# Vertical output matmuls as pairs of 128 rows by 64 columns

## The chip, the core and the metric

The kernel runs on one core of a Trainium2 chip. The metric is the device time of one execution in microseconds (us); lower is better. The core has five engines with queues of their own: TensorE (PE, matmuls, with its weight loads shown as PEld), VectorE (DVE), ScalarE (ACT), GpSimd (POOL) and SyncE (SP, which issues most of the DMAs). They run in parallel and wait for one another by semaphores.

## The reference: attention in horizontal and vertical stripes

An image of 224 x 224 tokens with 96 channels goes through one projection to q, k and v. The first 48 channels attend within horizontal stripes of 8 rows, the last 48 within vertical stripes of 8 columns; each kind has 28 stripes of 1,792 tokens. Both results are joined and multiplied by the output matrix `wo`.

```python
qkv = einsum('bhwc,cd->bhwd', x, wqkv)          # x 1x224x224x96, wqkv 96x288
# per horizontal stripe, channels 0..47; nh = 28 stripes of 8*224 tokens
ah = softmax(einsum('bqc,bkc->bqk', qh, kh) * 48**-0.5)
oh = einsum('bqk,bkc->bqc', ah, vh)
# per vertical stripe, channels 48..95; the same with qv, kv, vv -> ov
o  = concat(oh, ov)                              # written as two pads and a sum
return einsum('bhwc,cd->bhwd', o, wo)            # wo 96x96
```

Because `wo` acts on the 48 + 48 channels separately, the output is `oh @ wo[:48] + ov @ wo[48:]`. The kernel uses this: it finishes the horizontal part first, keeps it in SBUF, and adds it to the vertical part.

## The kernel before

**Tiling.** Two stripes are worked on together as a pair; there are 28 pairs, P = 0 to 13 horizontal and P = 14 to 27 vertical. Stripe w = 0 of a pair lives in partitions 0 to 63 and stripe w = 1 in partitions 64 to 127 of the tiles `QT_sb`, `KT_sb` and `OT_sb`. A pair's queries are cut into four chunks, of 512, 512, 512 and 256.

**Scores.** A unit is 128 keys by 512 queries (or twice 128 keys by 256) for both stripes of the pair. `qk_op` (L1015) computes a unit's scores with matmuls of 48 rows by 128 columns. In this text "rows" of a matmul are the partitions over which it sums, and "columns" the partitions of PSUM that it writes; the profile prints them as `48*128`. The two stripes' matmuls sit in different halves of the array's rows and are issued as a pair.

**Exponentials.** ACT takes 1,071 units with one activation each (L1037, PSUM to `PT`). DVE takes the other 301 (L1075 to L1094), with a part of the products on POOL.

**Values.** `pv_op` (L968) multiplies the probabilities by `V_sb`, with matmuls of 128 rows by 64 columns (`128*64` in the profile): stripe 0 writes PSUM partitions 0 to 63, stripe 1 partitions 64 to 127, and the two are again issued as a pair. `V_sb` has a column of ones behind the 48 channels, so row 48 of each result is the sum of the exponentials. DVE copies a finished chunk to `OT_sb` (L931).

**Output.** `fin` multiplies `OT_sb` by `wo`. For horizontal pairs (L809) a slot is a block of 64 tokens times one of the two stripes: the matmul has 128 rows by 64 columns and uses `wo_sb[0][w]`, a tile of 128 partitions that holds `wo` in the partitions of stripe w alone and zeros in the others. Two such matmuls, one for each stripe, fill the 128 partitions of a slot, and a group has 4 or 5 slots, so 8 or 10 matmuls of 97 moving columns. For vertical pairs a slot is 128 tokens of one stripe. With `rowed` set (L836, from the constant `VQ`, L372) the slot is a single matmul (L843) that sums over the 49 partitions of its stripe and writes all 128 partitions: `49*128`. A group again has 4 or 5 slots. Then DVE takes the reciprocal of the sums (L796), multiplies (L853), and POOL adds the horizontal part `Ph_sb` (L859); SP writes the output by DMA. One group, the last of all, is not `rowed` and runs as pairs at L847 in the kernel before too.

**Order.** The order of the work is written out as strings in `PLAN`, one for each engine: the string `"pe"` names by a digit the stream from which PE takes its next operation. Digits 1 and 2 are score units for ACT and for DVE, 3 and 4 are value products, 5 is an output group, 6 a projection for the next pair. `PLAN["bank"]` gives the PSUM banks in the same way. A planner (L167 to L343) walks through these strings, keeps an estimated clock, and so finds the waits and the buffers; ACT and SP have no string, and SP takes what the estimated clock has ready first. `mode` is a mark of each PE operation, "q" for the row form (L1018, and L913 for `rowed` groups) and "v" for the others; the planner's clock adds `SWITCH`, 0.099 or 0.117 us, where the mark changes. With the order given, it enters only this estimated clock.

In the string `"pe"`, the digits before and after each of the 84 `rowed` groups read as follows: 65 stand between a score unit and a value product or projection, 17 between two score units, and 2 between a value product and a score unit. None stands between two of the "v" kind.

Of the kernel before, what the change touches and what calls it, by code (L numbers as in the profile page):

```python
# [368 lines left out]
PRIO = (1, 0, 3, 5, 4, 2)  # L369
DPRIO = (0, 1, 2, 3)  # L370
HALVES = False
VQ = True  # L372
HB = [0, 5, 10, 15, 20, 24, 28]
VB = [0, 5, 10, 14]
LEAD, SPACE, PACE, FIRST = 8, 3, 0.9, 0
# [2 lines left out]
def bass_standalone__window_attn_cswin__vision_kernel(  # L378
# [30 lines left out]
    with es:  # L409
# [380 lines left out]
        def fin(P, c):  # L790
# [35 lines left out]
            else:  # L826
# [5 lines left out]
                for (k0, k1), ws in todo:  # L832
                    nk = k1 - k0
                    n = nk * len(ws)
                    last = P == NP - 1 and c == NCH - 1
                    rowed = VQ and len(ws) == 1  # L836

# [386 lines left out]
```

## Time and profile before

| | us |
|---|---|
| median of 3 runs | 1007.16 |
| lowest and highest | 1005.09, 1011.97 |
| the profiled execution | 1004.3 |
| its span, first to last instruction | 1002.5 |
| PE busy | 988.0 (99%) |
| ACT busy | 987.6 (99%) |
| DVE busy | 938.5 (94%) |
| POOL busy | 684.2 (68%) |
| granted TensorE clock | 0.999 of full |

The time of an execution is the span and 1.8 us around it. "Busy" is the union of the times in which an engine has an instruction in flight. Matmuls overlap: one with 512 moving columns is shown as some 380 ns, while the next pair starts some 215 ns after it. So a share of 99% doesn't mean that PE could do no more, and the pace is read from starts in the timeline and not from durations. In a row of the timeline, the first number is the start in us from the beginning of the span, the second how long the row's instructions are in flight together, and xN their count.

### The profile page before, as it was taken

The page shows a single profiled execution, that of the slowest core. Times are in us where ns is not written, and L with a number is a line of the kernel's source. Part 1 is how long each engine was busy: PE and PEld are TensorE (multiplying, and loading weights), DVE is VectorE, ACT ScalarE, POOL GpSimd, SP SyncE. Part 2 cuts the span into 40 slices and gives each one's busy share as a digit, 9 for nine tenths or more (in the row PEclk, how much of TensorE's full clock was granted, in tenths as well). Part 3 has the DMA queues.
Part 4 walks back from the last instruction along what each step waited for, and adds up shares of the span by engine and source line. Part 5 has one row for each costly group of instructions (what it writes and reads, how often), then busy time and mean ns, then how long its engine had stood idle before and what let it go on. Part 6 is the DMA issues. An engine that isn't in the chain of part 4 may idle for free.

```text
span 1002.5 us, 24560 instructions
## 1 busy us (share of the span) xinstructions
PE 988.0 (99%) x10211; PEld 385.9 (38%) x10211; DVE 938.5 (94%) x1573; ACT 987.6 (99%) x1080; POOL 684.2 (68%) x660
## 2 busy tenths in 40 slices
PE   8999999999999999999999999999999999999997
PEld 3433433343343334334334333433433443343342
DVE  8999999999999999999899999999999999999997
ACT  7999999999999999999999999999999999999997
POOL 3676766667677676777776776776676777677652
PEclk9999999999999999999999999999999999999999
DMA  5102120220112023011111122222122221222012
GB/s 110 39 2 38 38 32 8 38 38 1 39 39 32 8 38 38 2 36 25 27 29 32 25 46 50 54 52 44 34 41 52 53 54 39 52 52 40 13 36 50
DMA packets 164712, 36.92 MB, mean 37 GB/s; under 512 B 164488, under 2 KB 164488, under 8 KB 164600
## 3 DMA queue, kind: packets, MB, share of 16 engines
q1 hardware_dynamic: 163016, 34.80, 18.5%
q8 instruction: 80, 1.31, 0.5%
q10 hardware_dynamic: 1584, 0.55, 0.2%
q14 instruction: 32, 0.26, 0.1%
HBM read 0.44 MB, written 9.63 MB: 10 GB/s over the span
## 4 chain that ended last, share of the span: by engine, by line
ACT 70%; PE 29%; DVE 1%; issue 0%
ACT PT L1037 70%; PE ps L968 13%; PE ps L1015 11%; PE ps L686 2%; PE ps L761 1%; PE ps L843 1%; PE ps L532 0%; PE ps L809 0%; DVE OT_sb L931 0%; PE ps L647 0%; DVE out_sb L866 0%; DVE I_sb L1075 0%; DVE E_sb L1090 0%; DVE U_sb L1088 0%; PE ps L679 0%
## 5 line engine op out<-in xcount | busy, mean ns | idle before, releaser
L1037 ACT ACTIVATE PT<-ps 128x1024 bf16<-128x1024 f32 x1071 | 983.5, 1119 | 2.9 <-PE ps L1015 1.5
L1094 POOL TENSOR_TENSOR G_sb<-I_sb,U_sb 128x512 bf16<-128x512 bf16 x482 | 544.0, 1153 | 250.7 <-DVE E_sb L1090 225.3
L1015 PE MATMUL ps<-QT_sb,KT_sb 48*128 48x512 bf16 (+1 forms) x3136 | 463.0, 356 | 4.7 <-ACT PT L1037 3.0
L1075 DVE TENSOR_SCALAR I_sb<-ps 128x1024 int16<-128x1024 f32 x301 | 367.3, 1220 | 24.6 <-PE ps L1015 21.1
L968 PE MATMUL ps<-PT,V_sb 128*64 128x512 bf16 (+1 forms) x2422 | 363.8, 363 | 1.1 <-ACT PT L1037 1.0
L1015 PEld LDWEIGHTS ps<-QT_sb,KT_sb 48*128 48x128 bf16 x3136 | 123.2, 93 | 307.4 <-ACT PT L1037 223.7
L968 PEld LDWEIGHTS ps<-PT,V_sb 128*64 128x64 bf16 x2422 | 119.2, 109 | 122.5 <-issue 94.9
L968 PE MATMUL ps<-G_sb,V_sb 128*64 128x512 bf16 (+1 forms) x714 | 115.6, 356 | 0.0
L968 PE MATMUL ps<-E_sb,V_sb 128*64 128x512 bf16 (+1 forms) x714 | 109.9, 356 | 0.6 <-DVE OT_sb L931 0.2
L1088 DVE TENSOR_SCALAR U_sb<-I_sb 128x2048 int16<-128x2048 int16 (+1 forms) x161 | 109.2, 678 | 0.2
L859 POOL TENSOR_TENSOR out_sb<-tmp,Ph_sb 128x480 bf16<-128x480 f32 (+1 forms) x84 | 84.9, 1026 | 30.0 <-DVE E_sb L1090 10.7
L1090 DVE TENSOR_SCALAR E_sb<-I_sb 128x2048 int16<-128x2048 int16 (+1 forms) x161 | 104.9, 652 | 0.2 <-PE ps L968 0.2
L686 PE MATMUL ps<-xT_sb,w_sb 96*64 96x512 bf16 (+1 forms) x444 | 77.6, 367 | 0.9 <-ACT PT L1037 0.5
L931 DVE CAST OT_sb<-ps 128x512 bf16<-128x512 f32 x112 | 69.3, 619 | 5.9 <-PE ps L968 5.0
L706 DVE TENSOR_SCALAR_CACHE_REDUCE KT_sb<-ps 128x512 bf16<-128x512 f32 x110 | 67.8, 620 | 7.4 <-PE ps L686 6.8
L700 DVE TENSOR_SCALAR QT_sb<-ps 128x512 bf16<-128x512 f32 (+1 forms) x111 | 68.1, 619 | 5.2 <-PE ps L686 4.1
L766 DVE CAST V_sb<-ps 128x480 bf16<-128x480 f32 (+2 forms) x85 | 51.7, 611 | 3.1 <-PE ps L761 2.8
L968 PEld LDWEIGHTS ps<-G_sb,V_sb 128*64 128x64 bf16 x714 | 36.4, 108 | 47.3 <-issue 28.8
L720 POOL TENSOR_SCALAR KT_sb<-KT_sb,negmean 128x1792 bf16<-128x1792 bf16 x27 | 47.5, 1759 | 10.3 <-DVE E_sb L1090 6.2
L816 DVE TENSOR_TENSOR Ph_sb<-ps,rc 128x480 bf16<-128x480 f32 (+1 forms) x84 | 52.2, 622 | 2.1
L853 DVE TENSOR_TENSOR tmp<-ps,rc 128x480 f32<-128x480 f32 (+1 forms) x84 | 51.9, 618 | 2.2
L968 PEld LDWEIGHTS ps<-E_sb,V_sb 128*64 128x64 bf16 x714 | 33.9, 108 | 43.1 <-issue 21.1
(47 smaller groups left out, 324.4 us busy)
## 6 DMA issues: line engine op xcount, KB each, us to landing
out_dram<-out_sb SPq DMA_DIRECT2D x208, 42.0 KB, 2.1
xT_sb<-in_x_dram SPq DMA_TRANSPOSE x251, 2.4
out_dram<-out_sb SPq DMA_DIRECT2D x22, 24.0 KB, 1.9
Ph_sb<-in_x_dram ACTq DMA_DIRECT2D x1, 336.0 KB, 3.0
out_dram<-out_sb ACTq DMA_DIRECT2D x6, 24.0 KB, 1.9
wo_sb<-in_wo_dram SPq DMA_DIRECT2D x4, 9.0 KB
wo_sb<-one_sb SPq DMA_DIRECT2D x4, 0.0 KB
w_sb<-in_wqkv_dram ACTq DMA_DIRECT2D x1, 54.0 KB, 4.6
```

The costliest lines, as they stand in the source:

```text
L686: ins = e.matmul(bk[64 * w:64 * w + 64, 0:qs], lhsT=w_sb[0:C, wblk(P, kind), :], rhs=rhs, start=True, stop=True)
L700: return e.tensor_scalar(dst, src, QS, None, ALU.mult)
L706: return e.tensor_scalar(dst, src, 1.0, None, ALU.mult, ALU.add, accum_out=acc)
L859: return e.tensor_tensor(out_sb[b][:, k0:k0 + nk, ws[0], :], t, Ph_sb[:, k0:k0 + nk, j0 + ws[0], :], ALU.add)
L931: return e.tensor_copy(OT_sb[b][:, q0:q0 + qs], bk[:, 0:qs])
L968: return e.matmul(bank(k.bank)[64 * w:64 * w + 64, x0:x1], lhsT=lhs(w, kts[i])[p0:p1], rhs=rhs(w, i, qs)[p0:p1, x0:x1], start=(op.tok["fir ...
L1015: ins = e.matmul(bank(op.tok["s"][w])[:, i * qs:(i + 1) * qs], lhsT=KT_sb[b][64 * w:64 * w + C2, kt * 128:(kt + 1) * 128], rhs=QT_sb[b][64 ...
L1037: a.fn = lambda e: e.activation(PT[a.tok["p"]][:].rearrange("p (s n) -> p s n", s=2), two(q.tok["s"]), ACTF.Exp, scale=LN128)
L1075: return e.tensor_scalar(dst[:, at:at + 1024].rearrange("p (s n) -> p s n", s=2), two(src), 128.0 * ONE, 0.0, ALU.add, ALU.max)
L1088: f.fn = lambda e: e.tensor_scalar(U_sb[y()][:, 0:m], I_sb[y()][:, 0:m], M_FRAC, HALF, ALU.bitwise_and, ALU.bitwise_or)
L1090: x2.fn = lambda e: e.tensor_scalar(E_sb[x2.tok["l"]][:, 0:m], I_sb[y()][:, 0:m], M_EXP, E_LOW, ALU.bitwise_and, ALU.bitwise_or)
L1094: g.fn = lambda e: e.tensor_tensor(G_sb[x2.tok["l"]][:, i0:i1], I_sb[y()][:, i0:i1].bitcast(BF16), U_sb[y()][:, i0:i1].bitcast(BF16), ALU. ...
```

## The change

The constant `VQ` becomes false, so `rowed` is false for all vertical groups.

```diff
-VQ = True
+VQ = False
```

What this selects lies in `fin`:

```python
rowed = VQ and len(ws) == 1
...
    if rowed:                                   # before: one of 49 rows, 128 columns (L843)
        ins = e.matmul(bk3[:, s, :], lhsT=OT_sb[b][64 * w:64 * w + CA, t0:t0 + 128], rhs=wo_sb[1][w][64 * w:64 * w + CA, :], ...)
        continue
    for p0 in (0, 64):                          # after: two of 128 rows, 64 columns (L847)
        ins = e.matmul(bk3[p0:p0 + 64, s, :], lhsT=OT_sb[b][:, t0 + p0:t0 + p0 + 64], rhs=wo_sb[1][w][:, :], ...)
...
p, ops = fill((0.05 if rowed else 0.043) * n, pe_fn, ...)
if rowed:
    p.mode = "q"
```

The 388 matmuls of the 84 groups become 776, each with its weight load; the two of a slot write the lower and the upper 64 partitions of the same PSUM bank. They read all 128 partitions of `OT_sb`, and the zeros in `wo_sb[1][w]` take the other stripe out. The order of the operations, the banks, and what a group waits for (the copies of its chunk to `OT_sb`, and a free bank) stay. The planner's estimated clock changes a little, by 0.007 us a slot and by where the mark changes.

## The prediction
> **What bounds the kernel now.** I begin with the page: the busy shares, the chain that ended last, and the group of the exponentials.
>
> ```profile
> span 1002.5 us, 24560 instructions
> ...
> PE 988.0 (99%) x10211; PEld 385.9 (38%) x10211; DVE 938.5 (94%) x1573; ACT 987.6 (99%) x1080; POOL 684.2 (68%) x660
> ...
> ACT 70%; PE 29%; DVE 1%; issue 0%
> ...
> L1037 ACT ACTIVATE PT<-ps 128x1024 bf16<-128x1024 f32 x1071 | 983.5, 1119 | 2.9 <-PE ps L1015 1.5
> ```
>
> Three engines are nearly full, and busy shares alone don't choose between them. The chain does: 70% of the span lies on ACT and 29% on PE. ACT's exponentials sat idle for 2.9 us in the whole run. So ACT sets the pace, and PE sets it in short stretches where ACT has caught up with the scores. The next view gives busy time by stretches: one of the horizontal half, then one of the vertical half, where the change acts (the number behind x is a count of instructions).
>
> ```profile
> 300.00:400.00 100.00, 99.59 (x1088) 38.64 (x1086) 92.45 (x153) 100.00 (x111) 70.22 (x66) 1.00 0.21 28
> ...
> 600.00:700.00 100.00, 99.11 (x966) 38.58 (x964) 96.52 (x162) 99.56 (x110) 70.15 (x69) 1.00 0.25 50
> ```
>
> The fourth group of figures is ACT: 111 instructions in 100 us in one stretch and 110 in the other, one every 0.90 to 0.91 us, although one is in flight for 1.12 us. The horizontal half runs its output groups in the form that the change brings to the vertical half, and ACT goes there at the same pace or a little quicker. That speaks against a large loss; it proves nothing, since DVE has less to do there (92% against 97%). Third, the waits:
>
> ```profile
> PEld ps L1015 <- ACT PT L1037: 223.7, 696, 0.8
> ...
> PE ps L1015 <- ACT PT L1037: 3.0, 9, 1.0
> ...
> DVE rc L796 <- PE ps L843: 1.4, 5, 0.5
> ```
>
> Score units waited 696 times for ACT to give back a PSUM bank: mostly it is PE that is ready first. A weight load that waits isn't yet an idle array (only 9 such waits, 3.0 us, stopped the matmuls themselves), so PE has slack in small pieces, and there is little to spare. DVE waited for a vertical output group in only 5 of 84 cases.
>
> **The change, part by part.** First the matmuls themselves, grouped by line and form, new form (L809, in the horizontal half) and old form (L843):
>
> ```profile
> L809 PE MATMUL ps<-wo_sb,OT_sb 128*64 128x97 bf16 x784 | 32.3, 210 | 0.0
> L843 PE MATMUL ps<-wo_sb,OT_sb 49*128 49x97 bf16 x388 | 30.5, 203 | 0.0
> ...
> L843 PEld LDWEIGHTS ps<-wo_sb,OT_sb 49*128 49x128 bf16 x388 | 24.7, 94 | 12.7 <-DVE KT_sb L706 1.2 <-DVE OT_sb L931 1.0 <-ACT PT L1037 0.9
> L809 PEld LDWEIGHTS ps<-wo_sb,OT_sb 128*64 128x64 bf16 x784 | 23.7, 109 | 18.6 <-issue 7.1 <-DVE V_sb L766 2.2 <-DVE OT_sb L931 1.6
> ```
>
> Twice as many instructions of the new form keep PE busy for about the same time, 32.3 us against 30.5 us, for 392 and 388 slots: the two of a slot run side by side. What differs is what stands before and behind a group. The timeline of PE shows both forms between a score unit and a value product (65 of the 84 groups), the new form here, in groups of five slots:
>
> ```profile
> 280.81 0.39 PE L1015 MATMUL ps<-QT_sb,KT_sb 48*128 48x512 bf16 x2
> 281.13 0.41 PE L809 MATMUL ps<-wo_sb,OT_sb 128*64 128x97 bf16 x10
> 281.37 0.38 PE L968 MATMUL ps<-PT,V_sb 128*64 128x512 bf16 x2
> ```
>
> The old form, from the vertical half:
>
> ```profile
> 667.09 0.39 PE L1015 MATMUL ps<-QT_sb,KT_sb 48*128 48x512 bf16 x2
> 667.31 0.38 PE L843 MATMUL ps<-wo_sb,OT_sb 49*128 49x97 bf16 x5
> 667.62 0.41 PE L968 MATMUL ps<-G_sb,V_sb 128*64 128x512 bf16 x2
> ```
>
> In the old form the group starts 0.22 us behind the score pair and the value pair 0.31 us behind the group: 0.53 us in all. In the new form it is 0.32 and 0.24: 0.56 us. PE pays some 0.1 us where it goes from 48- or 49-row matmuls to 64-column ones; the change moves this price from behind the group to before it. The 0.03 us that remain come back at once: the first pair after such a step is in flight for 0.41 us instead of 0.38, and in the old form that is the value pair, in the new one the group. I count these 65 groups at nothing; uncovered they would be 65 x 0.03 = 2.0 us. The 2 groups between a value product and a score unit have one step in either form: nothing.
>
> Between two score units (17 groups) the old form has no step and the new one has two. Groups of four slots, the new form:
>
> ```profile
> 295.79 0.61 PE L1015 MATMUL ps<-QT_sb,KT_sb 48*128 48x512 bf16 x4
> 296.33 0.36 PE L809 MATMUL ps<-wo_sb,OT_sb 128*64 128x97 bf16 x8
> 296.63 0.39 PE L1015 MATMUL ps<-QT_sb,KT_sb 48*128 48x512 bf16 x2
> ```
>
> The old form at such a place:
>
> ```profile
> 647.82 0.61 PE L1015 MATMUL ps<-QT_sb,KT_sb 48*128 48x512 bf16 x4
> 648.26 0.34 PE L843 MATMUL ps<-wo_sb,OT_sb 49*128 49x97 bf16 x4
> 648.45 0.39 PE L1015 MATMUL ps<-QT_sb,KT_sb 48*128 48x512 bf16 x2
> ```
>
> From the same start the next score unit begins after 0.84 us in the new form and after 0.63 us in the old: 0.21 us more. Over 17 groups that is 17 x 0.21 = 3.6 us of work on PE, all between 526 and 993 us: the first of the 17 follows.
>
> ```profile
> 525.80 0.61 PE L1015 MATMUL ps<-QT_sb,KT_sb 48*128 48x512 bf16 x6
> 526.24 0.38 PE L843 MATMUL ps<-wo_sb,OT_sb 49*128 49x97 bf16 x5
> 526.54 0.39 PE L1015 MATMUL ps<-QT_sb,KT_sb 48*128 48x512 bf16 x2
> ```
>
> And one that shows what hides this work:
>
> ```profile
> 935.17 0.60 PE L1015 MATMUL ps<-QT_sb,KT_sb 48*128 48x512 bf16 x4
> 935.62 0.33 PE L843 MATMUL ps<-wo_sb,OT_sb 49*128 49x97 bf16 x4
> 936.08 0.39 PE L1015 MATMUL ps<-QT_sb,KT_sb 48*128 48x512 bf16 x2
> ```
>
> At 935 us the next score unit came 0.91 us after the first, because its bank wasn't free; the new form, with 0.84 us, fits into that and costs nothing. At 526 and 648 us there was no wait, and the whole step is new. So PE's delay lies between 0 and 3.6 us, nearer to the upper end, as most of the places look like 648.
>
> How much of this reaches the end? Where ACT still has a finished unit in front of it, a score unit that is 0.2 us late is not missed, and PE catches up at its next wait for a bank. Where PE is on the chain, the delay stays. I take the chain's own share: 29% of the span lies on PE, so 0.29 x 3.6 = 1.0 us. The ends are kept for the range: nothing, and the whole 3.6 us.
>
> There is one gain to set against it. Where a group itself waits for its inputs for longer than the step takes, the step before it is hidden and the step behind it is gone: 0.1 us each. In the timeline I find three such groups between 526 and 993 us (at 529, 719 and 753 us), so some 0.4 us at most comes back. Nothing changes in DMA, POOL or SP work: no transfer is added or moved. DVE runs the same instructions, but gets a group's result later: the group's last slot begins at 0.32 + 0.20 = 0.52 us behind the score pair instead of 0.22 + 0.18 = 0.40 us (the time in flight less one matmul's 0.21 or 0.20). These 0.12 us matter only where DVE arrives just then; the 5 waits of 84 give 5 x 0.12 = 0.6 us on DVE, which is not the chain's engine. It is late next if that count is far too low.
>
> The sum, against the profiled execution: 1004.3 (span 1002.5 and 1.8 around it) + 1.0 = 1005.3 us. That execution lies 2.9 us below the median of the runs shown, so I put the same 1.0 us on the median: 1007.16 + 1.0 = **1008.2 us**.
>
> A rule of the Trainium skill speaks against the change. "TensorEngine Tiling (Array Packing)", section "Gotcha 2: Feature Incompatibilities", says that column tiling excludes Fast Weight Load, and "TensorE: Matmul & The Clock Gate", section "Weight-path perf modes — Fast Weight Load (FWL) and DoubleRow", gives that faster load to 128-column weights alone: the old form could have it and the new one not. This trace agrees in sign (94 ns a load in the old form, 109 ns for half as many columns in the new), but not in effect, since the loads at L809 lie beside running matmuls. What a form that pays for its loads would cost is the second rival.
>
> **The rivals.**
>
> 1. *DVE arrives in time more often than its waits show* (slower). DVE works in order and is 97% busy in this half; if it stood before every one of the 82 groups whose step moves ahead of them, it would lose 82 x 0.12 = 9.8 us, its reads of score units behind the group would free their banks later, and PE's units for ACT would wait on these. With PE's 3.6 us: 1004.3 + 13.4 = 1017.7 us, 1.3% more. It decides from the point at which DVE's spare time, some 3.5 us in 100, is used up. For it speaks that share; against it that DVE waited at L796 only 5 times for 1.4 us. Chance 0.06.
> 2. *Weight loads show* (slower). If the new form's loads stood in PE's way, each slot would cost one load of 109 ns more: 388 x 0.109 = 42 us, 1046 us. The rows of L809 speak against it: ten matmuls with ten loads start within 0.20 us. In the vertical half the tiles are the same in size and lie in the same memory. Chance 0.01.
> 3. *Nothing reaches the end*: ACT hides all of it, 1004.3 us, or 1007.2 as a median. For it: the 696 waits of PE for ACT. It is in the range and in the same class as the forecast. Chance 0.30.
> 4. *The change does more than its matmuls*: the planner's clock shifts by 0.007 us a slot and by the marks, and SP, which takes its order from that clock, could exchange a load and a store, or a buffer be handed out in another order. The order of PE, DVE and POOL and the banks are written out, so I see no way to more than 2 us in either direction, except by a store that holds back a load at a pair's beginning. Chance 0.05, of it 0.01 for over 1% slower and 0.01 for over 1% faster.
>
> **How the numbers follow.** The forecast (0.2 to 3.6 us slower) has a chance of 0.58, the rivals 0.06, 0.01, 0.30 and 0.05. About 1% is what a measurement of this kernel can tell from no change, as its runs lie from 1005.09 to 1011.97. Slower by over 1%: 0.06 + 0.01 + 0.01 = 0.08. Faster by over 1%: 0.01, and 0.01 more for what I don't see, 0.02. Within 1%: 0.90. The range takes the profiled run less the gain of 0.4 us as its lower end, 1003.9, and the highest run with the PE delay less its hidden part, 1011.97 + 2.0, as its upper end, 1014.0.
>
> **What would show it.** The timeline after should have pairs at L847, ten in some 0.41 us, each 0.32 us behind a score pair, and score units behind 17 of them some 0.34 us later. The 526 us before the first vertical group should be unchanged. Waits of DVE at L796 for L847 should stay under some 5 us; 10 us and more would be the first rival. ACT's pace should stay at about 110 in 100 us; 108 throughout would mean a loss that I haven't priced. I'd be wrong altogether if the two matmuls of a slot ran one after the other in this half.

## The result, and the profile after

The changed kernel takes 1009.82 us as the median of 20 runs (1006.93 to 1011.79), the kernel before 1006.35 us as the median of its 20 runs in the same comparison: a ratio of 1.003 with a 95% interval from 1.0019 to 1.0042, some 3 us more. By the bound of 1% that is no change; by the interval it is slower.

The profiled execution of the changed kernel took 1011.51 us. The page of it, with the busy shares, the chain and the exponentials:

```profile
span 1009.6 us, 25334 instructions
...
PE 992.4 (98%) x10599; PEld 382.4 (38%) x10599; DVE 940.8 (93%) x1573; ACT 990.0 (98%) x1080; POOL 684.9 (68%) x660
...
ACT 59%; PE 36%; DVE 2%; SPq 2%; issue 1%; DMA 0%; POOL 0%
...
L1037 ACT ACTIVATE PT<-ps 128x1024 bf16<-128x1024 f32 x1071 | 986.0, 1105 | 8.5 <-PE ps L1015 6.4
```

Before its exponentials ACT sat idle for 8.5 us in place of 2.9, and 6.4 us of it were for scores of PE; PE has 36% of the chain in place of 29%. Not all of the 7.1 us between the two spans belongs to the change. The view of busy time by stretches shows the first 20 us of the kernel before and then of the changed one (the third number from the end is PE's granted clock):

```profile
0.00:20.00 20.00, 17.43 (x159) 7.82 (x159) 16.04 (x41) 14.24 (x20) 5.65 (x17) 1.00 0.56 122
```

```profile
0.00:20.00 20.00, 17.09 (x141) 7.03 (x143) 13.52 (x37) 11.93 (x18) 5.55 (x17) 0.83 0.45 99
```

The clock at the beginning was 1.00 in the one and 0.83 in the other, and both values come up in traces of kernels of either kind. In the trace of the changed kernel the clock was at half for 6.8 of these 20 us:

```profile
12.30:19.10 6.80, 6.65 (x28) 2.03 (x28) 4.29 (x8) 5.00 (x6) 2.61 (x3) 0.50 0.00 0
```

The last output matmul of the horizontal half (L809), which the change doesn't touch, starts at 510.2 to 511.1 us in the traces with 1.00 in the first 20 us, at 512.4 in the one with 0.91, and at 513.3 to 513.8 in those with 0.83 (leaving out one kernel below, whose added waits lie in this half too). So I measure the vertical stretch, from the last matmul of L809 to the last of L847, which holds all that the change touches. The lines' own view gives first and last starts, here of the kernel before:

```profile
L809 PE MATMUL ps<-wo_sb,OT_sb x784: 205/207/232, 27.5 to 511.1; 128*64 128x97 bf16 x196
...
L847 PE MATMUL ps<-wo_sb,OT_sb x8: 207/207/231, 996.6 to 996.7; 128*64 128x97 bf16 x8
```

And of the changed kernel:

```profile
L809 PE MATMUL ps<-wo_sb,OT_sb x784: 205/207/231, 30.2 to 513.8; 128*64 128x97 bf16 x196
...
L847 PE MATMUL ps<-wo_sb,OT_sb x784: 207/207/231, 529.0 to 1004.4; 128*64 128x97 bf16 x196
```

Before: 996.7 - 511.1 = 485.6 us. After: 1004.4 - 513.8 = 490.6 us, 5.0 us more. Behind the last group the changed kernel needs 5.2 us to the end of the span and the kernel before 5.8, so 4.4 us remain. The changed kernel entered the stretch 2.7 us later, which is what the traces above show to go with the clock.

The matmuls do what the prediction's rows said. Timeline of PE after the change, a group between a score unit and a value product, and the group that stood at 648 us:

```profile
670.42 0.39 PE L1015 MATMUL ps<-QT_sb,KT_sb 48*128 48x512 bf16 x2
670.74 0.41 PE L847 MATMUL ps<-wo_sb,OT_sb 128*64 128x97 bf16 x10
670.98 0.38 PE L968 MATMUL ps<-G_sb,V_sb 128*64 128x512 bf16 x2
```

```profile
650.83 0.38 PE L1015 MATMUL ps<-QT_sb,KT_sb 48*128 48x512 bf16 x2
651.14 0.36 PE L847 MATMUL ps<-wo_sb,OT_sb 128*64 128x97 bf16 x8
651.43 0.39 PE L1015 MATMUL ps<-QT_sb,KT_sb 48*128 48x512 bf16 x2
```

The group of ten comes 0.32 us behind the scores and the value pair 0.24 us behind it, 0.56 us in all; the group of eight needs 0.31 + 0.29 = 0.60 us from the last score pair to the next one.

But three other things stand in this trace that the prediction didn't price. First, instructions of DVE that should take 0.68 us take up to 1.78 us. Timeline of DVE and of POOL at one place, before:

```profile
874.82 0.68 DVE L1094 TENSOR_TENSOR G_sb<-I_sb,U_sb 128x1024 bf16<-128x1024 bf16 x1
```

```profile
876.88 1.76 POOL L720 TENSOR_SCALAR KT_sb<-KT_sb,negmean 128x1792 bf16<-128x1792 bf16 x1 [2.68 <-DVE E_sb L1090]
```

And after:

```profile
880.41 1.78 DVE L1094 TENSOR_TENSOR G_sb<-I_sb,U_sb 128x1024 bf16<-128x1024 bf16 x1
```

```profile
879.90 1.76 POOL L720 TENSOR_SCALAR KT_sb<-KT_sb,negmean 128x1792 bf16<-128x1792 bf16 x1
```

Before, POOL waited for an instruction of DVE and came behind the product. After, it doesn't wait, is under way when the product begins, and the product ends at 882.19, 0.53 us behind POOL's end at 881.66. The same stands at 657 us (0.68 becomes 1.18), at 887 us (0.69 becomes 1.15) and at 898 us (0.69 becomes 1.58). Second, PE stops before a projection of the next pair:

```profile
684.79 0.41 PE L968 MATMUL ps<-PT,V_sb 128*64 128x256 bf16 x4
686.55 0.41 PE L686 MATMUL ps<-xT_sb,w_sb 96*64 96x512 bf16 x2 [1.35 <-issue]
```

The kernel before has no such stop there. The projection needs the next pair's loads, and the timeline of SP shows where the last one stands, behind 16 stores:

```profile
645.14 26.22 SPq L558 DMA_TRANSPOSE xT_sb<-in_x_dram  x19
671.40 10.92 SPq L887 DMA_DIRECT2D out_dram<-out_sb  x16
682.36 18.10 SPq L558 DMA_TRANSPOSE xT_sb<-in_x_dram  x13
```

The first of the 13 loads behind the stores, issued at 682.36, is the last one that the projection needs. Third, the order of SP there is another one: 19 loads stand ahead of these stores, and 18 did before.

### The profile page after: what moved, and what is told of

Read it like the earlier page. It is cut to its first block, busy times and chain, and to the rows that moved or that the text cites. A ratio compares the mean times of both kernels' runs of the same rounds, so it can differ in the third digit from the quotient of the medians.

```text
span 1009.6 us, 25334 instructions
## 1 busy us (share of the span) xinstructions
PE 992.4 (98%) x10599; PEld 382.4 (38%) x10599; DVE 940.8 (93%) x1573; ACT 990.0 (98%) x1080; POOL 684.9 (68%) x660
## 3 DMA queue, kind: packets, MB, share of 16 engines
q8 instruction: 83, 1.36, 0.6%
## 4 chain that ended last, share of the span: by engine, by line
ACT 59%; PE 36%; DVE 2%; SPq 2%; issue 1%; DMA 0%; POOL 0%
ACT PT L1037 59%; PE ps L968 16%; PE ps L1015 14%; PE ps L686 2%; SPq L887 2%; PE ps L847 1%; PE ps L761 1%; DVE I_sb L1075 1%; DVE G_sb L1094 0%; PE ps L532 0%; PE ps L809 0%; DVE tmp L853 0%; DVE OT_sb L931 0%; DVE E_sb L1090 0%; DVE QT_sb L700 0%
## 5 line engine op out<-in xcount | busy, mean ns | idle before, releaser
L686 PE MATMUL ps<-xT_sb,w_sb 96*64 96x512 bf16 (+1 forms) x444 | 77.8, 367 | 2.7 <-issue 1.4
```

What stands on the lines that cost most here:

```text
L686: ins = e.matmul(bk[64 * w:64 * w + 64, 0:qs], lhsT=w_sb[0:C, wblk(P, kind), :], rhs=rhs, start=True, stop=True)
```

## Experiments

Theory A: the steps between matmul forms are the price. Theory B: the order of SP's queue, which the planner lays down by its clock. Theory C: the planner's clock also decides for which instruction of DVE a POOL instruction waits, and weaker waits let both engines meet. The planner does this with `vlock` (L209 to L212, L224 to L229): a POOL instruction marked `lock` gets a wait for the marked DVE instruction that was placed last in the planner's clock. Comparing the instruction lists of both kernels shows that the order of PE, ACT, DVE and POOL is the same, and that all of the plan's difference lies in nine waits of POOL, each for an earlier DVE instruction than before, and in one load on SP that changed places with the 16 stores.

All kernels compute the whole reference. "Stretch" is the vertical stretch.

### The parts of the change, one at a time

In the first two, `rowed` chooses the matmul and a new name `as_row` what the planner is told.

```diff
-                    rowed = VQ and len(ws) == 1
+                    rowed, as_row = False, len(ws) == 1
...
-                    p, ops = fill((0.05 if rowed else 0.043) * n, pe_fn, evs + [op_w],
+                    p, ops = fill((0.05 if as_row else 0.043) * n, pe_fn, evs + [op_w],
...
-                    if rowed:
+                    if as_row:
                         p.mode = "q"
```

**New matmuls, old plan.**

> All vertical groups are pairs of 128 rows by 64 columns, but the planner is told the old cost and the old mark, so that SP's order and every buffer are those of the kernel before. The vertical half is measured from the last matmul of L809 to the last of L847: 485.6 us before, 490.6 us after the change. Theory A (the steps between matmul forms are the price: 17 groups, up to 3.6 us on PE): the half stays at 488 us or above, and the time is 2 to 3 us over the kernel before. Theory B (the order of SP is the price): the 1.35 us stop of PE before L686 near 686 us is gone and the half falls to 486 us, the time to that of before. Theory C (the new pace makes DVE and POOL instructions meet that did not meet before, so that DVE instructions of 0.7 us take 1.2 to 1.8 us): the half is still above 487 us and the stretched DVE instructions of the changed kernel stand again near 657, 880 and 898 us, or at other places.

Measured: ratio 1.0001 (0.9987 to 1.0015). The stretch took 1001.5 - 513.5 = 488.0 us, 2.4 us over before. The long DVE instructions near 657, 880, 887 and 898 us are gone, those of the kernel before are there. The stop before L686 is still there (1.19 us), although SP's order is the old one: theory B isn't right in the form in which I put it.

**Old matmuls, new plan** (`rowed, as_row = len(ws) == 1, False`).

> All vertical groups keep one matmul of 49 rows by 128 columns, but the planner is told the new cost and the new mark, so that SP's order and the buffers are those of the changed kernel. Theory A: the same as before, 485.6 us for the vertical half. Theory B: PE stops some 1.3 us before a projection near 683 us, because the last load of the next pair stands behind 16 stores, and the half takes about 487 us, +1.3 us in the time. Theory C: 485.6 us plus what a stop of PE sets off behind it.

Measured: ratio 1.0007 (0.9986 to 1.0029). The stretch took 999.5 - 510.3 = 489.2 us, 3.6 us over before with not one matmul changed. The long DVE instructions are there, at 654, 876, 883 and 893 us, and a stop of 1.09 us before L686. Theory A alone has fallen.

**New matmuls in the 17 groups alone.** The two neighbours of a group are read from the plan string; the plan is the old one.

```diff
-VQ = True
+FIVES = iter([i for i, ch in enumerate(PLAN["pe"]) if ch == "5"][84:])
...
-                    rowed = VQ and len(ws) == 1
+                    five = next(FIVES); between = PLAN["pe"][five - 1] in "12" and PLAN["pe"][five + 1:five + 2] in ("1", "2"); rowed, as_row = len(ws) == 1 and not between, len(ws) == 1
```

> Only the 17 groups between two score units are pairs of 64 columns, the other 67 keep the old form, and the plan is that of the kernel before. Theory A: all of PE's price is here, so the half takes as long as with all 84 groups changed and the plan of before (2 us or more over 485.6 us). Theory B: no change. Theory C: about 1 us from the steps alone and more where instructions of DVE and POOL meet, at places that need not be those of the changed kernel.

Measured: ratio 0.9984 (0.9971 to 0.9997), though the stretch took 997.6 - 511.0 = 486.6 us, 1.0 us more than before, with 0.18 us of a stop before L686 in it. A time below that of before with a longer stretch shows how far the beginning and the end of an execution weigh; I go by the stretch.

**New matmuls in the other 67 groups** (`rowed = len(ws) == 1 and between`).

> Only the 67 groups beside a value product or projection are pairs of 64 columns, the 17 between two score units keep the old form, and the plan is that of the kernel before. Theory A: nothing, 485.6 us for the half, since the step only moves from behind the group to before it; if the later result (0.12 us) mattered to DVE, up to 3 us more. Theory B: nothing. Theory C: within 0.5 us of before, unless the shift of 0.1 us in a group is enough to make a DVE and a POOL instruction meet.

Measured: ratio 1.0003 (0.9986 to 1.002). The stretch took 997.7 - 510.2 = 487.5 us. The stop before L686 is 1.49 us here and delays the next scores by 1.7 us; without it some 0.2 us remain over 485.6. So a step that moves from behind a group to before it costs next to nothing, and the later results didn't hold up DVE.

### The waits of POOL

**The changed kernel with the nine old waits.**

```diff
-        pl.run()
+        pl.run(); [pl.out["pool"][i][0].append((SEMS["dve"], n)) for i, n in ((434, 947), (508, 1111), (511, 1117), (583, 1278), ...)]
```

> The changed kernel, with nine waits of POOL put back. In the changed plan nine POOL instructions wait for an earlier instruction of DVE than in the plan of before (the first is an addition at L859 that waits for DVE's 940th instruction and not for its 947th); here they wait for both, and SP's order stays that of the changed plan. Theory C (the weaker waits let POOL run into DVE's products): the DVE instructions of 1.2, 1.8, 1.1 and 1.6 us that the changed kernel has near 657, 880, 887 and 898 us are gone, and the vertical half, from the last matmul of L809 to the last of L847, falls from 490.6 us to about 488.3 us, of which up to 1.7 us may be a stop of PE before L686 near 684 us. Theory A (only the steps between matmul forms count): 490 us as in the changed kernel. Theory B (the order of SP's load and stores): 490 us with the stop near 684 us.

Measured: ratio 1.0021 (1.0005 to 1.0037). The stretch took 1001.6 - 513.4 = 488.2 us, 2.4 us less than the changed kernel, with a stop of 1.36 us in it. The product of the fence above takes its old time again:

```profile
879.60 0.68 DVE L1094 TENSOR_TENSOR G_sb<-I_sb,U_sb 128x1024 bf16<-128x1024 bf16 x1
```

Its SP order is that of the changed kernel, and it stands within 0.2 us of the kernel with the old order: that order is worth 0.2 us at most.

**The kernel before with the nine new waits**, put in the place of the old ones in the same manner.

> The kernel before with the nine weaker waits of POOL of the changed plan, and with nothing else of it: old matmuls, old order of SP. Theory C: long DVE instructions near 654, 876, 882 and 893 us, and the half is 2.0 to 2.3 us over 485.6 us, apart from the stop before L686. Theory A and theory B: 485.6 us apart from that stop.

Measured: ratio 1.0009 (0.9995 to 1.0023). The stretch took 999.1 - 511.0 = 488.1 us, 2.5 us more, with no stop before L686: it is the waits alone. Timeline of DVE and POOL:

```profile
875.33 1.78 DVE L1094 TENSOR_TENSOR G_sb<-I_sb,U_sb 128x1024 bf16<-128x1024 bf16 x1
```

```profile
874.82 1.76 POOL L720 TENSOR_SCALAR KT_sb<-KT_sb,negmean 128x1792 bf16<-128x1792 bf16 x1
```

So theory C holds, from both sides, at 2.4 to 2.5 us.

**More waits.** In the trace of before, 21 DVE instructions are stretched by a POOL instruction that is under way when they begin, by 5.8 us together. Here each of these POOL instructions waits for that DVE instruction too.

> The kernel before, in which each of the 21 POOL instructions that stretch a DVE instruction in its trace also waits for the end of that DVE instruction (and of the SBUF-to-SBUF ones right behind it). Theory C: the 5.8 us by which those DVE instructions are too long go, and if POOL's later products reach PE in time the kernel is 1 to 3 us faster than before; if PE waits for these products, it is the same or slower. Theory A and theory B say nothing of it: the same time as before, as DVE isn't on the chain.

Measured: ratio 1.0191 (1.0171 to 1.0212), 19 us slower. A wait of the kernel before, and then the waits of this one:

```profile
PEld ps L968 <- POOL G_sb L1094: 3.9, 12, 0.4
```

```profile
PEld ps L968 <- POOL G_sb L1094: 21.0, 29, 1.9
...
ACT PT L1037 <- PE ps L1015: 18.8, 29, 1.8
```

PE's weight loads waited 21.0 us for POOL's products (3.9 us in the kernel before), ACT 18.8 us for scores, and new meetings took the place of the old ones (4.8 us). Not all of the 19 us are these waits. In this trace PE's clock was at half once more in the middle of the kernel, for 13.7 us, and the exponentials fell back by 5.6 us there:

```profile
899.80:913.50 13.70, 13.70 (x108) 4.88 (x102) 8.47 (x13) 9.21 (x9) 5.39 (x5) 0.50 0.23 46
```

The five executions were granted a mean clock of 0.987 to 0.992. At 0.991 and 0.992 this kernel is 13.5 and 12.3 us slower than executions of the kernel before with the same clock. Whether the waits bring the lower clock with them isn't shown. Even 12 us are more than the 5.8 us that the meetings took: a meeting is cheaper here than keeping a late POOL waiting.

### The load, the kernels once more, and more steps

**The kernel before once more.**

> The kernel before once more, to see how much its own trace changes from one execution to the next. Theory B: the last load for the next pair reaches L686 near 682 us in time, as in the first trace, and PE doesn't stop there. If PE stops there for 0.4 to 1.7 us in this kernel too, this stop belongs to the kernel before as well and is no part of the change. The half without that stop is 485.6 us in any case, and the long DVE instructions stand at the same places as in the first trace.

Measured: 1007.00 us. The stretch took 999.4 - 513.7 = 485.7 us with no stop, and every score unit behind 526 us starts within 0.12 us of its place in the first trace, apart from the 2.7 us of the beginning.

**The changed kernel once more.**

> The changed kernel once more. Theory C: the long DVE instructions stand at the same four places as in its first trace and the half is 490.6 us, or down to 489.1 us if the stop before L686 is shorter this time. If they were accidents of that execution, the half is near 487 us.

Measured: 1010.95 us. The stretch took 1003.9 - 513.3 = 490.6 us, with the four long DVE instructions and a stop of 1.38 us. They aren't accidents.

**Two loads ahead of the stores, new matmuls and old plan otherwise.**

```diff
-        pl.run()
+        pl.run(); pl.out["sp"][194:212] = pl.out["sp"][210:212] + pl.out["sp"][194:210]
```

> All vertical groups as pairs of 64 columns with the plan of before, and on SP the last two loads of the seventh vertical pair stand ahead of the 16 stores and not behind them. If the stop of PE before L686 near 684 us (1.4 us with the same kernel and the old queue) comes from these two loads standing behind the stores, it is gone, and the half, from the last matmul of L809 to the last of L847, is what the steps alone cost: 486.6 us, 1.0 us over before. If the stop has another cause it stays and the half is 488.0 us.

Measured: ratio 0.9988 (0.9969 to 1.0006). The stretch took 996.9 - 510.2 = 486.7 us, and PE doesn't stop at the projection:

```profile
680.72 0.41 PE L968 MATMUL ps<-PT,V_sb 128*64 128x256 bf16 x4
680.96 0.39 PE L686 MATMUL ps<-xT_sb,w_sb 96*64 96x512 bf16 x2
```

The stop is a wait for those loads, and without it and the meetings the new matmuls cost 486.7 - 485.6 = 1.1 us.

**The same loads, old matmuls.**

> The kernel before with the two loads ahead of the 16 stores. Its two traces had no stop there, so the trace should stay as it is, 485.6 us for the half. If some executions of the kernel before do stop for these loads, the median falls by a part of a microsecond; if the later stores hold back POOL's additions, it rises.

Measured: ratio 0.9966 (0.9948 to 0.9985), a median of 1004.98 us: the lowest ratio of all, 2.5 us below the kernel before in the same comparison (1007.48). The stretch is 999.3 - 513.6 = 485.7 us, as before; what the trace shows to be shorter is the end, 4.8 us behind the last group in place of 5.8. The timeline of SP at the end, before and then here:

```profile
996.52 2.91 SPq L887 DMA_DIRECT2D out_dram<-out_sb  x4
999.48 1.26 SPq L898 DMA_DIRECT2D out_dram<-out_sb  x2
```

```profile
999.16 1.32 SPq L887 DMA_DIRECT2D out_dram<-out_sb  x2
1000.52 1.43 SPq L898 DMA_DIRECT2D out_dram<-out_sb  x2
```

SP had two stores fewer left when the last group came. That the two exchanged loads, 320 us earlier, do this isn't shown: the end takes 4.8 us also in two kernels whose loads weren't exchanged (the new matmuls with the old plan, and the last kernel below). The other 1.5 us of the difference are the clock. The executions of this kernel were granted 0.995 to 0.999, those of the kernel before 0.990 to 0.999, 11 of 29 of them below 0.995. At 0.995 the means are 1006.1 (of 3) and 1007.1 us (of 8), at 0.998 they are 1002.9 (of 3) and 1004.1 us (of 3): 1.0 to 1.2 us are left.

**More steps in the 17 groups.** As in the experiment with the 17 groups alone, but slots 1 and 3 of each (slot 1 alone where a group has four) take the old form and the others the new one.

```diff
-                            if rowed:
+                            if rowed or (between and s in (1, 3) and s < n - 1):
```

> As with only the 17 groups between score units changed and the plan of before, but in these 17 the slots alternate between the two forms: 90 steps between forms in place of 34, so 90 x 0.1 = 9 us of work on PE. If the end takes PE's share of the chain (0.29), the half is 2.7 us over 485.6 us: 488.3 us. If the first 0.2 us of each place are hidden and what is beyond them goes straight through, it is 485.6 + 0.6 + 5.6 = 491.8 us. If new meetings of DVE and POOL come with it, it can be more than that.

Measured: ratio 1.0035 (1.0017 to 1.0053). The stretch took 1004.7 - 512.4 = 492.3 us, 6.7 us over before, with no stop before L686 and no new long instruction of DVE. That is 0.5 us over the second figure, and 4.0 us over the one by the share of the chain.

## Why the prediction was right, and where not

**The time** lies in the range, and the class, within 1%, was the likeliest. The median moved by 1009.82 - 1006.35 = 3.5 us where 1.0 was forecast; 3.5 lies at the upper end of the forecast's own 0.2 to 3.6.

**The steps between forms**: right in kind. Where they were counted at nothing (67 groups) 0.2 us was found, and the whole price of the new matmuls is 1.1 us where 1.0 was forecast. The 3.6 us of PE's delay were too many. With the new matmuls, and without stop and meetings, the next score pair starts 0.54 to 0.67 us behind the last one where one of the 17 groups has five slots, and 0.57 to 0.63 us where it has four. In the kernel before this took from 0.34 to 0.67 us, which fits a wait like that at 935 us at many of the places. Together the 17 places became 2.5 us longer, only 6 of them by 0.19 us or more. So "most of the places look like 648" was wrong. The gain of up to 0.4 us isn't seen: the places at 719 and 753 us became 0.12 and 0.21 us longer.

**How much of them reaches the end**: right in size by luck, wrong in kind. The first step that failed is "I take the chain's own share: 29%". Of the 2.5 us, 1.1 came out, so 1.4 were caught up behind the places. With more steps the same 17 places became 8.7 us longer and 6.7 came out, so 2.0 were caught up. By the share it would have been 0.7 and 2.5 us. Some 0.1 us behind each place is hidden in both kernels, and what is beyond goes through: of the 6.2 us that the second has over the first, 5.6 reach the end. The forecast met 1.1 us because its delay was too large and its share too small.

**"Nothing changes in DMA, POOL or SP work"**: this is the second step that failed, and it cost more. POOL's work doesn't change, but its waits do, and one load moves. Rival 4 named the cause, the planner's clock, and looked for it in SP's order and in buffers, with at most 2 us; it acted through nine waits of POOL and cost 2.4 to 2.5 us. SP's order, which was the effect that I named, was worth 0.2 us at most. The text before the prediction already said too much, that what the planner's mark does is only an estimated clock: the waits come out of that clock.

**A load that is just in time**: missed. SP issues 16 loads and 16 stores for each pair, and at 682 us the last load for the next pair stands behind the stores. In the two traces of the kernel before it landed 1.35 and 0.57 us before PE took it up; in those of the changed kernel PE stopped for 1.35 and 1.38 us. Moving the loads takes the stop away. The traces also show what makes this load late. The view of the DMAs gives its time from issue to landing, in the kernel before and in the changed one:

```profile
xT_sb<-in_x_dram SPq DMA_TRANSPOSE x1, 2.4
```

```profile
xT_sb<-in_x_dram SPq DMA_TRANSPOSE x1, 4.1
```

In the 2.2 us behind the issue the same view lists one packet of the kind "instruction" in the changed kernel (count, MB, share of the 16 engines), and none in the kernel before:

```profile
q8 instruction: 1, 0.02, 2.9%
```

Such a packet has 16 KB and is in flight for about 1 us. In nine of the fourteen traces one was in flight in that time, and there the load took 3.05 to 4.17 us to land; in the other five it took 2.35 to 2.40 (in two of these one began in the last 0.15 us before the load had landed). The old matmuls with the loads first are among the nine, with 3.87 us, and lost nothing, as the load came 9 us early there. The nine hold every trace in which all 84 or the 67 groups have the new matmuls and the load stands behind the stores, and also the old matmuls with the new plan. So, as far as these traces go, the stop is no price of the matmuls themselves: a load with little slack meets such a packet. What places these packets in time, and how many executions of either kernel have the stop, isn't shown.

**The sum.** Steps 1.1, meetings of DVE and POOL 2.4, the stop 1.5 (what a stop of 1.35 us shifts the next scores by): 5.0 us, as measured in the stretch of both traces. The three are differences between neighbouring kernels (486.7, 488.2 and 490.6 us), so they have to add up; what tests them is the old matmuls with the new plan, where 485.6 + 2.5 for the meetings + 1.1 for the stop give the 489.2 us that were measured. The end is 0.6 us shorter, so 4.4 us in the span behind the horizontal half. The medians differ by 3.5 us; the remaining 0.9 us isn't settled. Executions with the same mean granted clock differ by 3.8 us (means at 0.995, 1010.9 of 9 against 1007.1 of 24) and 3.6 us (at 0.999, 1007.9 of 4 against 1004.3 of 11); those of the kernel before are from the comparisons of the experiments.

Each stretch is read from one trace, or from two. The medians alone don't settle 1 or 2 us, since the clock moves them as much: a straight line through the times of the kernel before over their mean granted clock falls by 0.97 us for each 0.001. Measured from this line the changed kernel lies 3.5 us higher on average, and 1.5 us with the nine old waits put back; the kernel before lies 1.8 us higher with the nine new waits, and 5.6 us with more steps. So over all executions the nine waits are worth 2.0 us in the one and 1.8 in the other. Apart from the kernel with added waits, the figures from this line are smaller than those of the stretches by 0.7 to 1.5 us, of which the shorter ends make up 0.4 to 1.0.

**The rivals.** DVE waiting for later results: DVE's waits for a vertical group rose to 9 with 3.0 us from 5 with 1.4, far from 9.8 us. Weight loads that show: no; L847 runs like L809.

```profile
DVE rc L796 <- PE ps L847: 3.0, 9, 0.5
```

```profile
L847 PE MATMUL ps<-wo_sb,OT_sb 128*64 128x97 bf16 x784 | 33.2, 212 | 0.7 <-DVE OT_sb L931 0.7
```

Of the Trainium skill, the rule on fast weight load in "TensorEngine Tiling (Array Packing)", section "Gotcha 2: Feature Incompatibilities", made no difference here, as L809 had let one expect. Another page describes what did: "SBUF — State Buffer", section "Who interferes with whom", says that DVE and GpSimd share a pair of ports as an exclusive lock, and that the instruction that is issued first holds it to its end, against a DVE instruction in a two-port mode or with two SBUF inputs. The traces agree: each stretched DVE instruction ends a fixed 0.53 to 0.55 us (0.28 us where it has half the elements) behind the POOL instruction that it met.

## What to carry to other kernels

Where a planner writes the waits, a change of its costs or marks is a change of the program: compare the instruction lists and the waits of all engines, not the edited engine alone, and give the planner the old figures once, to see what the edit itself is worth. A price on an engine with small slack was hidden here by some 0.1 us behind each place, and not by a share; look at every place before counting on the price of one. Measure such a change between two marks of the trace, as the beginning of an execution here varies by as much as the change is worth, and compare times at the same granted clock. Where an engine stops for a load, look at what else the DMAs carried before it landed.

## What was not expected of the hardware

PE's clock in the first 20 us was granted at 1.00 in one trace of the kernel before and at 0.83 in the other, and moved the whole trace by 2.7 us. Behind that the two traces repeat within 0.1 us over 480 us, down to the DVE instructions that a POOL instruction stretches: at the same three places they are 0.61, 0.57 and 0.47 us too long in every trace, to 0.01 us, but in that with the added waits. A packet of the kind "instruction" that met a load made it land 0.7 to 1.8 us later.
